# Batch 0's sine sums inside the thirds of x, step 1's P product ahead of step 0's Q product, joint E's last places two steps apart

## Chip, cores and metric

The kernel runs on one core of one Trainium2 chip. The metric is the device time of one execution in microseconds (us): the median over several runs. The core has five engines that work side by side, each through its own instructions in order: TensorE (PE in the profile; PEld are its weight loads), VectorE (DVE), ScalarE (ACT), GpSimd (POOL) and SyncE (SP), which here only issues DMAs. Matmul results land in PSUM, of which there are eight banks; all else is in SBUF.

## What is computed

```python
X = np.fft.fft(x, axis=1)            # x: (8, 3008, 256) float32
X = np.fft.fft(X, axis=2).real       # only the real part goes on
x = X.reshape(8 * 3008, 256)
gate = 1.0 / (1.0 + np.exp(-(x @ w_gate)))   # w_gate, w_val: (256, 1536)
val = x @ w_val
out = (gate * val) @ w_out                   # w_out: (1536, 256)
```

The three weights come in 64-bit floats and are turned into 32-bit ones on the chip. All matmuls are in 32-bit floats; each shows as two matmul pieces in the profile.

## The kernel before

**The algebra.** The transform over the 256 features is merged into the gate and value weights once: `merge` multiplies each chunk of 256 weight columns by the table `dt` and leaves the products in `G1` and `G2`. The transform over the 3008 rows is a cosine sum P (`pk`) and a sine sum Q (`qk`) over folded rows of x; a row k and its mirror row come out of the same two products, as G1·P plus and minus G2·Q. One feature (number 128) has its own cosine sums, called E (`er`, `ed`): they are added to the products through `ge`, in batch 0's first steps through a small matmul with `e0`.

**Batch 0's start** (lines 813 to 869). The rows of x come as a tile `X[0]` of 128 partitions with six slots q in each; the table `ST` holds, for each slot, the cosines and sines of 753 frequencies: first 377 even ones (NE), then 376 odd ones (NO). SP issues the loads in program order on one queue: two weight chunks, then three times two slots of x and the cosines of the same slots (lines 820 to 822), then the sines of slots 0 to 2 and of slots 3 to 5 (lines 823 and 824), then eight more weight chunks. A *third* is two slots. For each third `half_rows` (line 461) folds x on DVE (lines 405, 409, 418, 469, 471), and PE then runs the E sums (`pe`) and the cosine sums of both blocks: block 0 are the even, block 1 the odd frequencies, each in two PSUM tiles, `ev` and `od`, for even and odd slots. After the last third `then` (line 507) copies `ev` to SBUF on ACT (line 518), and `places` puts sum and difference of `ev` and `od` into `pk` with two DVE instructions (lines 524 and 528). The sine sums come after all thirds: slots 0 to 2 of block 0, then of block 1, then slots 3 to 5 of both (lines 857 to 860). Their results are placed into `qk` between the parts of weight chunks 2, 3 and 5.

**Weight chunks.** `weight_parts` is two ACT instructions (lines 296 and 297), `weight_join` three on DVE (306, 307, 309) and one on POOL (311), `weight_use` calls `merge`: four matmuls into a tile `ps` (eight pieces), two ACT copies (331, 332) and small DMAs. The order of chunks by `jobs` is such that step 0 uses chunk 2, step 1 chunks 3 and 5, step 2 chunk 6, step 3 chunk 8.

**Steps.** The main loop (line 942) has 576 steps; a step is one of 12 feature tiles f for one chunk of 252 rows k (six chunks in a batch). Step i has, in order of issue: `front_a` (PE: G1·P of gate and value into the bank `PF[i]`, and in steps 0 to 4 the E product with `e0` too), `gate_a(i-1)` (ACT 658, DVE 659), `part` (ACT 644: a copy of twice G1·P, into `ae`), `seed` (ACT 629: E for the next step), `gate_b(i-1)` (DVE 671, ACT 672, weight joins, DVE 675, POOL sums 681), `back` (PE: output products of step i−5), `front_b` (PE: G2·Q onto the same bank, which needs `part` to have read it), weight uses, then `n` entries from the list `later`, which `finish` fills every 12 steps with 24 entries (DVE sums, line 765, transposes, line 773, and stores), then whatever `at` put into `side` for this step.

**Joint E.** Steps 40 to 43 compute the E sums of the other seven batches: `e_joint` in step 40 (24 matmul pieces, two copies, two places), a copy in step 41, one place (line 524) in step 42, and the other place (line 528) and the store to `ed` in step 43.

Of the kernel before, what the change touches and what calls it, by code (L numbers as in the profile page):

```python
# [53 lines left out]
NQ = 6  # L54
NP = 128
# [26 lines left out]
def kernel(  # L82
# [10 lines left out]
    nc = tc.nc  # L93
    B, _, _, _, D = xf.shape
# [5 lines left out]
    NE = (M // 2) // 2 + 1  # L100
    NO = (M // 2) // 2
# [8 lines left out]
    N3 = NQ // 2  # L110
# [64 lines left out]
    ST = [const.tile([P, 2, NQ, NE + NO], F32, name="st", tag="st")]  # L175
# [11 lines left out]
    def load_rows(q, n):  # L187
        nc.sync.dma_start(out=X[0][0:NP, :, q : q + n], in_=xf[0, :, :, q : q + n])

    def load_table(t, q, n):  # L190
        nc.sync.dma_start(out=ST[0][0:NP, t, q : q + n], in_=stab[:, t, q : q + n])

    def table_again():

# [47 lines left out]
    def weight_load(j):  # L242


        w, c = jobs[j]
        src = (moe_w_gate, moe_w_val, moe_w_out)[w]
        src = src[2 * c * P : 2 * (c + 1) * P, :] if w == 2 else src[:, c * WC : (c + 1) * WC]
        src = src.rearrange("(c p) f -> p c f", p=P)

        def some(n, pool, tag):  # L250

            if tag not in shared:
                shared[tag] = pool.tile([P, n * WC], F32, name=f"w{tag}", tag=tag)
            return shared[tag]

        def home(j):

            if j in (0, 1, 2, 3, 5):
                if j > 2:
                    ws = some(5, pqp, "qk")[:, (j // 5) * 2 * WC : (j // 5 + 1) * 2 * WC]  # L260
                    return sp.tile([P, 4 * WC], F32, name="raw", tag="sf"), ws
                t = hp.tile([P, 6 * WC], F32, name="raw", tag="h")
                return t[:, 0 : 4 * WC], t[:, 4 * WC :]
            if j in (4, 6, 9):
                t = wf[:, {4: 1, 6: 2, 9: 3}[j]].rearrange("p m n -> p (m n)")
                return t[:, 0 : 4 * WC], t[:, 4 * WC : 6 * WC]
            t = some(10, cp, "c")
            if j == 7:
                raw = pqp.tile([P, 4 * WC], F32, name="raw", tag="pk")
                return raw, t[:, 6 * WC : 8 * WC]  # L270
            return t[:, 0 : 4 * WC], t[:, 4 * WC : 6 * WC]

        if j < KEEP:
            raw, ws = home(j)
        else:
            both = some(24, xp, "x4").rearrange("p (i n) -> p i n", n=2 * WC)
            r, i = (j - KEEP) % 3 * 2, 6 + (j - KEEP) % 6
            raw, ws = both[:, r : r + 2].rearrange("p a n -> p (a n)"), both[:, i]
            if w == 2:
                i = (0, 0, 8, 0, 2, 4)[c] * WC  # L280
                ws = some(10, cp, "c")[:, i : i + 2 * WC]
        raw = raw.bitcast(I32).rearrange("p (c f w) -> p c f w", c=2, w=2)
        ws = ws.rearrange("p (c f) -> p c f", c=2)
        WS[j] = ws
        if src.dtype == F32:
            nc.sync.dma_start(out=ws, in_=src)
        else:
            RAW[j] = raw
            nc.sync.dma_start(out=raw.rearrange("p c f w -> p c (f w)"), in_=src.bitcast(I32))

    def weight_parts(j):

        if j in RAW:
            raw, ws = RAW[j], WS[j]
            lo, hi = raw[:, :, :, 0], raw[:, :, :, 1]
            nc.scalar.activation(ws, hi.bitcast(F32), AF.Abs)
            nc.scalar.activation(lo, lo.bitcast(U32), AF.Copy, scale=2.0 ** -29)

    def weight_join(j):
        if j not in RAW:  # L300
            return
        raw, ws = RAW.pop(j), WS[j]
        lo, hi = raw[:, :, :, 0], raw[:, :, :, 1]
        wi = ws.bitcast(I32)
        ts = nc.vector.tensor_scalar
        ts(out=ws, in0=ws, scalar1=2.0 ** -15, scalar2=HUGE, op0=ALU.max, op1=ALU.min)
        ts(out=wi, in0=wi, scalar1=3, scalar2=0x3FFFFFF8, op0=ALU.logical_shift_left,
           op1=ALU.bitwise_and)
        nc.vector.scalar_tensor_tensor(out=wi, in0=hi, scalar=-(2 ** 30), in1=wi,
                                       op0=ALU.bitwise_and, op1=ALU.bitwise_or)  # L310
        nc.gpsimd.tensor_tensor(wi, wi, lo, op=ALU.add)
# [229 lines left out]
    def seq_group(b, blk, what, other=None):  # L541
        return half(b, lambda q: W[b, blk][what][:, q, :], PQE[b][what], blk, what == 1, other)
# [14 lines left out]
    def e_sums(m=B - 1):  # L557


        ps = bank("pe", NB - 1)  # L560
        at_ = lambda blk, par: slice((2 * blk + par) * TB, (2 * blk + par) * TB + m)

        def sums(*qs):
            for q in qs:
                for blk in range(2):
                    c0, n = ((0, NE), (NE, NO))[blk]
                    w = x8[:, :, 1 + 2 * blk, q] if m > 1 else W[0, blk][2][:, q]
                    mm(ps[at_(blk, q % 2), 0:n], w, ST[0][0:NP, 0, q, c0 : c0 + n], q < 2, q >= NQ - 2)

        def even():  # L570
            er = op.tile([P, NK + 1], F32, name="er", tag="os")[0:m]
            if m == 1:
                E0.append(er)
            nc.vector.memset(er[:, NK:], 0.0)
            a = evp.tile([P, 2 * NJ], F32, name="a", tag="a")[0:m, 0:NE]
            e1 = evp.tile([P, 2 * NJ], F32, name="a", tag="a")[0:m, 0:NE]
            nc.scalar.copy(a, ps[at_(0, 1), 0:NE])
            nc.scalar.copy(e1[:, 0:NO], ps[at_(1, 0), 0:NO])

            places(er, 0, True, a, ps[at_(0, 0), 0:NE])  # L580

            def rest():
                nc.scalar.copy(a[:, 0:NO], ps[at_(1, 1), 0:NO])

            def last():
                places(er, 1, False, e1[:, 0:NO], a[:, 0:NO], (0,))

            def end():
                places(er, 1, False, e1[:, 0:NO], a[:, 0:NO], (1,))
                nc.sync.dma_start(out=ed[1:] if m > 1 else ed[0:1], in_=er)  # L590
            return rest, last, end
        return sums, even
# [38 lines left out]
    def front_a(i):  # L631
        (pk, *_), ks, _, _, fs = cut(i)
        if i < N1:
            seed(i)
        for g in range(2):
            mm(PF[i][:, g], G1[:, g, fs], pk[:, ks], i < N1 and g == 0, True)
        for g in range(2 if i < N1 else 0):
            mm(PF[i][:, g], G2[:, g, fs], e0, False, True)

    def part(i):  # L640

        n = cut(i)[2]
        AP[i] = app.tile([P, 2, CH], F32, name="ae", tag="ae")[:, :, 0:n]
        nc.scalar.activation(AP[i], PF[i], AF.Copy, scale=2.0)  # L644
# [175 lines left out]
    for q in range(0, NQ, 2):  # L820
        load_rows(q, 2)
        load_table(0, q, 2)
    for q in range(0, NQ, N3):
        load_table(1, q, N3)
    for j in (2, 3, 5, 6, 8, 9, 4, 7):
        weight_load(j)

# [12 lines left out]

    cos = [seq_group(0, blk, 0, (2 * blk, 2 * blk + 1)) for blk in range(2)]
    e_, e_even = e_sums(1)
    for i, f in enumerate(fold_ops(0, 2)):
        q = 2 * i, 2 * i + 1
        f()
        e_(*q)
        cos[0][0](*q)
        cos[1][0](*q)
    cos[0][1]()()
    cos[1][1]()()  # L850
    rest, *ends = e_even()
# [2 lines left out]
    for f in ends:  # L854
        f()
    nc.scalar.copy(e0[0:1], E0[0][:, 0:CH])
    sin = [seq_group(0, blk, 1, (0, 1) if blk else None) for blk in range(2)]
    for q in range(0, NQ, N3):
        for sums, _, _ in sin:
            sums(*range(q, q + N3))  # L860
    for j in range(KEEP, KEEP + 3):
        weight_load(j)
    weight_join(2)
    weight_parts(3)
    sin[0][1]()()
    weight_parts(5)
    sin[1][1]()()
    weight_join(3)
    e_rows(0)
# [4 lines left out]
    def at(i, *fs):  # L874
        side.setdefault(i, []).extend(fs)
# [18 lines left out]
    i0 = NFT  # L894
    count = 3 * len(groups)
# [7 lines left out]
    later_e = []  # L903
# [1 line left out]
    at(3 * i0 + 5, lambda: later_e[0]())  # L905
    at(3 * i0 + 6, lambda: later_e[1]())
    at(3 * i0 + 6, table_again)
    at(3 * i0 + 7, lambda: later_e[2]())
    at(4 * i0 - 3, lambda: [at(i, f) for i, f in zip((50, 46, 48, 49, 51, 52), table_odd())])
    for i in range(i0, count, i0):  # L910
        at(i - (8 if i == i0 else 11), lambda i=i: e_rows(i))
# [28 lines left out]
    at((B - 2) * per + 4 * i0 + 8, lambda: [at((B - 2) * per + 4 * i0 + 9 + 2 * i, f) for i, f in enumerate(plain_ops())])  # L940

    for i in range(count):
        front_a(i)
        if i:
            gate_a(i - 1)
        part(i)
        if N1 <= i + 1 < count:
            seed(i + 1)
        if i:
            gate_b(i - 1, *join.pop(i, []))  # L950
        for f in pre.pop(i, []) + out_use.pop(i, []):
            f()
        if i >= 5:
            back((i - 5) // 3, (i - 5) % 3)
        merges = use.pop(i, [])
        for f in merges[0 : min(i, 1)]:
            f()
        front_b(i)
        for f in merges[min(i, 1) :]:
            f()  # L960
        n = 3 if i >= count - 8 else 2 + i % 2
        for f in later[0:n]:
            f()
        del later[0:n]
        for f in side.pop(i, []):
            f()
# [55 lines left out]
```

## Time and profile before

| what | value |
|---|---|
| runs, median (lowest to highest) | 1925.85 us (1925.78 to 1925.87) |
| profiled execution | 1925.74 us, of it the span on the core 1924.0 us |
| PE busy | 1910.2 us, 99% |
| DVE, ACT, POOL busy | 1430.1, 1343.0, 1522.6 us |
| 15 to 34 us (folding and sums of batch 0) | PE 17.66 of 19.0 us, DVE 14.91, DMA engines busy throughout, 399 GB/s |
| 34 to 48 us (steps 0 to 2) | PE 13.32 of 14.0 us, DVE 11.71, ACT 8.61, POOL 5.29 |
| 180 to 200 us (steps 40 to 45) | PE 18.81 of 20.0 us, DVE 16.17, POOL 17.58 |

How to read it: a busy share is the time in which the engine had an instruction at work, and says nothing of which engine the others wait for. That is told by the idle time of the engine that is on the path, with what ended each piece of it; the tables by stage show where engines are close to full. In the profile's lines a tile is named by its name in the program without its number, so `pf` is any `PF[i]`, and a matmul is written `out<-moving,stationary`. Line 134 is the helper that issues every matmul.

### The profile page before, as it was taken

What the parts mean: (1) busy time and instruction counts of PE and PEld (TensorE: products, weight loads), DVE (VectorE), ACT (ScalarE), POOL (GpSimd) and SP (SyncE); (2) the same over time, 40 slices, a digit from 0 to 9 for tenths busy, and PEclk for the clock granted to TensorE, in tenths of its full rate; (3) what the DMA queues carried; (4) which work ended last, traced back from release to release, by engine and by line L of the source; (5) the groups of instructions that cost most, each with busy time, mean ns of one, the idle gap of its engine ahead of it and who ended that gap; (6) DMA issues with size and microseconds to landing.
All of it is one profiled execution on the core that took longest, in us unless ns stands there. A gap on an engine that the chain in (4) does not pass through costs nothing.

```text
span 1924.0 us, 34205 instructions
## 1 busy us (share of the span) xinstructions
PE 1910.2 (99%) x11164; PEld 1776.2 (92%) x11164; DVE 1430.1 (74%) x3225; ACT 1343.0 (70%) x3148; POOL 1522.6 (79%) x2733
## 2 busy tenths in 40 slices
PE   8999999999999999999999999999999999999999
PEld 5789999999999999999999999999999999999998
DVE  7677877787777777777777777777777687777775
ACT  4877767767777677776777767777677767777775
POOL 2389969978898788986888878888788986877770
PEclk9999999999999999999999999999999999999999
DMA  8353222221131211202111121121200100011001
GB/s 312 106 99 74 72 80 57 51 66 29 20 77 26 80 18 35 70 14 80 26 47 50 20 82 21 47 51 24 80 15 15 26 16 15 14 21 21 15 17 31
DMA packets 172321, 97.02 MB, mean 50 GB/s; under 512 B 134397, under 2 KB 162792, under 8 KB 170096
## 3 DMA queue, kind: packets, MB, share of 16 engines
q1 hardware_dynamic: 171566, 94.32, 20.2%
q8 instruction: 90, 1.47, 0.3%
q14 instruction: 87, 0.71, 0.1%
q10 hardware_dynamic: 546, 0.51, 0.1%
q0 software_dynamic: 32, 0.00, 0.0%
HBM read 70.08 MB, written 46.71 MB: 61 GB/s over the span
## 4 chain that ended last, share of the span: by engine, by line
PE 97%; DVE 1%; ACT 0%; DMA 0%; issue 0%; SPq 0%
PE pf L134 51%; PE po L134 42%; PE ev L134 3%; PE ps L134 1%; PE od L134 1%; DMA raw<-in_moe_w_val_dram 0%; DVE c L765 0%; DVE x L418 0%; DVE x L469 0%; DVE z L659 0%; ACT ae L644 0%; PE pe L134 0%; ACT pf L672 0%; ACT wl L389 0%; DVE x L409 0%
## 5 line engine op out<-in xcount | busy, mean ns | idle before, releaser
L681 POOL TENSOR_TENSOR sf<-h 128x168 f32<-128x168 f32 (+1 forms) x920 | 510.2, 573 | 218.9 <-DVE h L675 218.6
L681 POOL TENSOR_TENSOR sf<-h,sf 128x168 f32<-128x168 f32 (+1 forms) x1104 | 614.8, 577 | 56.2 <-DVE h L675 55.7
L134 PE MATMUL pf<-qk,G 128*128 128x252 f32 (+1 forms) x2304 | 582.1, 375 | 1.9 <-ACT ae L644 1.9
L134 PE MATMUL pf<-pk,G 128*128 128x252 f32 (+1 forms) x2304 | 582.7, 376 | 0.0
L675 DVE TENSOR_TENSOR h<-pf,z 128x252 f32<-128x252 f32 (+1 forms) x576 | 241.6, 419 | 418.8 <-ACT pf L672 418.8
L629 ACT ACTIVATE pf<-ek,ge 128x252 f32<-128x252 f32 (+1 forms) x1142 | 538.0, 471 | 20.4 <-DMA ge<-G 1.1
L134 PE MATMUL po<-sf,wf 128*128 128x168 f32 (+1 forms) x2944 | 508.2, 305 | 0.0
L644 ACT ACTIVATE ae<-pf 128x504 f32<-128x504 f32 (+1 forms) x576 | 339.2, 589 | 237.7 <-PE pf L134 236.5
L134 PEld LDWEIGHTS pf<-pk,G 128*128 128x128 f32 x2304 | 436.8, 190 | 52.5 <-issue 2.3
L134 PEld LDWEIGHTS po<-sf,wf 128*128 128x128 f32 x2944 | 453.3, 190 | 8.0
L134 PE MATMUL po<-h,wf 128*128 128x168 f32 (+2 forms) x2584 | 459.7, 306 | 0.0
L134 PEld LDWEIGHTS pf<-qk,G 128*128 128x128 f32 x2304 | 411.0, 190 | 32.3 <-ACT ae L644 3.1
L765 DVE TENSOR_TENSOR c<-c 128x168 f32<-128x168 f32 (+1 forms) x920 | 431.0, 501 | 4.8
L134 PEld LDWEIGHTS po<-h,wf 128*128 128x128 f32 x2584 | 411.5, 190 | 17.0 <-issue 0.9
L659 DVE TENSOR_TENSOR z<-ae,pf 128x504 f32<-128x504 f32 (+1 forms) x576 | 383.7, 666 | 35.3 <-ACT h L658 33.7
L658 ACT ACTIVATE h<-pf 128x252 f32<-128x252 f32 (+1 forms) x576 | 217.8, 378 | 164.5 <-PE pf L134 158.7
L672 ACT ACTIVATE pf<-z 128x252 f32<-128x252 f32 (+1 forms) x576 | 214.0, 372 | 78.1 <-DVE h L671 75.0
L671 DVE TENSOR_TENSOR h<-h,pf 128x252 f32<-128x252 f32 (+1 forms) x576 | 232.9, 404 | 0.0
L681 POOL TENSOR_TENSOR sf<-sf 128x168 f32<-128x168 f32 (+1 forms) x184 | 105.5, 573 | 14.4
L681 POOL TENSOR_TENSOR sf<-sf,h 128x168 f32<-128x168 f32 (+1 forms) x184 | 100.3, 545 | 0.0
L748 ACT COPY c<-po 128x504 f32<-128x504 f32 (+1 forms) x138 | 78.4, 568 | 0.0
L773 DVE STREAM_TRANSPOSE os<-c 128x256 f32<-128x256 f32 x188 | 72.2, 422 | 0.4 <-issue 0.3
(139 smaller groups left out, 899.1 us busy)
## 6 DMA issues: line engine op xcount, KB each, us to landing
x<-xr SPq DMA_DIRECT2D x14, 1536.0 KB
out_dram<-os SPq DMA_DIRECT2D x368, 56.0 KB
xr<-in_xf_dram SPq DMA_DIRECT2D x14, 768.0 KB
xr<-in_xf_dram SPq DMA_DIRECT2D x35, 256.0 KB
ek<-ed SPq DMA_DIRECT2D x40, 126.0 KB
out_dram<-os SPq DMA_DIRECT2D x284, 7.0 KB
x<-in_xf_dram SPq DMA_DIRECT2D x3, 1024.0 KB
st<-in_stab_dram SPq DMA_DIRECT2D x3, 753.0 KB
```

Of the source, the lines that this page charges most:

```text
L134: nc.tensor.matmul(o, l, r, start=start, stop=stop, skip_group_check=True)
L629: nc.scalar.activation(PF[i][:, g], EK[i // NFT], AF.Copy, scale=ge[:, g, f : f + 1])
L644: nc.scalar.activation(AP[i], PF[i], AF.Copy, scale=2.0)
L658: nc.scalar.activation(H[p][:, fh, 0:n], PF[i][:, 0], AF.Sigmoid)
L659: nc.vector.tensor_tensor(z[:, :, ::-1], AP.pop(i), PF[i], op=ALU.subtract)
L671: nc.vector.tensor_tensor(h[:, fh, 0:n], h[:, fh, 0:n], pf[:, 1], op=ALU.mult)
L672: nc.scalar.activation(pf[:, 0], z[:, 0], AF.Sigmoid)
L675: nc.vector.tensor_tensor(h[:, fh, n:], pf[:, 0], z[:, 1], op=ALU.mult)
L681: nc.gpsimd.tensor_tensor(block(p, dst), block(p, a), block(p, b), op=(ALU.subtract, ALU.add)[op])
L748: (nc.vector.tensor_copy if t == 1 or t == 3 else nc.scalar.copy)(C[0][:, 3 * t * R : 3 * (t + 1) * R], PO[t][:, 0 : 3 * R])
L765: nc.vector.tensor_tensor(t[:, dst * R : (dst + 1) * R], *v, op=(ALU.subtract, ALU.add)[op])
L773: nc.vector.transpose(os_[0][:, s, 0:nb, h, :], t[:, c0 : c0 + nb * TB])
```

## The change

Three places of batch 0 are edited, and the table's loads with them.

The sines are loaded by blocks: behind the cosines of each two slots come the sines of the even block (377 columns) for the same slots, and the sines of the odd block (376 columns, all six slots) come in one load behind the last of these. Block 0's sine sums are run in each third, behind its cosine sums; block 1's sine sums follow after the thirds. The copy of block 0's sine sum on ACT is issued ahead of chunk 2's join, its two places on DVE behind it. Chunk 5's two ACT instructions move from ahead of block 1's places to behind `part(0)`.

In the loop `front_a(1)` is issued right behind `front_a(0)`, and step 1 has none.

Joint E's last place and its store go from step 43 to step 44, and steps 43 and 45 take two entries of `later` where odd steps take three.

```diff
-    def load_table(t, q, n):
-        nc.sync.dma_start(out=ST[0][0:NP, t, q : q + n], in_=stab[:, t, q : q + n])
+    def load_table(t, q, n, lo=0, hi=NE + NO):
+        nc.sync.dma_start(out=ST[0][0:NP, t, q : q + n, lo:hi], in_=stab[:, t, q : q + n, lo:hi])
...
     for q in range(0, NQ, 2):
         load_rows(q, 2)
         load_table(0, q, 2)
-    for q in range(0, NQ, N3):
-        load_table(1, q, N3)
+        load_table(1, q, 2, 0, NE)
+    load_table(1, 0, NQ, NE)
     for j in (2, 3, 5, 6, 8, 9, 4, 7):
         weight_load(j)
...
     cos = [seq_group(0, blk, 0, (2 * blk, 2 * blk + 1)) for blk in range(2)]
     e_, e_even = e_sums(1)
+    sin = [seq_group(0, 0, 1)]
     for i, f in enumerate(fold_ops(0, 2)):
         q = 2 * i, 2 * i + 1
         f()
         e_(*q)
         cos[0][0](*q)
         cos[1][0](*q)
+        sin[0][0](*q)
...
-    sin = [seq_group(0, blk, 1, (0, 1) if blk else None) for blk in range(2)]
-    for q in range(0, NQ, N3):
-        for sums, _, _ in sin:
-            sums(*range(q, q + N3))
+    sin.append(seq_group(0, 1, 1, (0, 1)))
+    sin[1][0](*range(NQ))
     for j in range(KEEP, KEEP + 3):
         weight_load(j)
+    places_0 = sin[0][1]()
     weight_join(2)
+    places_0()
     weight_parts(3)
-    sin[0][1]()()
-    weight_parts(5)
     sin[1][1]()()
     weight_join(3)
     e_rows(0)
...
-    at(3 * i0 + 7, lambda: later_e[2]())
+    at(3 * i0 + 8, lambda: later_e[2]())
...
     for i in range(count):
-        front_a(i)
+        if i != 1:
+            front_a(i)
+        if i == 0:
+            front_a(1)
         if i:
             gate_a(i - 1)
         part(i)
+        if i == 0:
+            weight_parts(5)
...
-        n = 3 if i >= count - 8 else 2 + i % 2
+        n = 3 if i >= count - 8 else 2 + (i % 2 and i not in (3 * i0 + 7, 3 * i0 + 9))
```

## What I predict, before the changed kernel ran

> **Where the time is.** I read the page first, then the list of waits by engine, then the timeline of each engine over the two places that the waits point to.
>
> ```profile
> span 1924.0 us, 34205 instructions
> ...
> PE 1910.2 (99%) x11164; PEld 1776.2 (92%) x11164; DVE 1430.1 (74%) x3225; ACT 1343.0 (70%) x3148; POOL 1522.6 (79%) x2733
> ...
> PE 97%; DVE 1%; ACT 0%; DMA 0%; issue 0%; SPq 0%
> ```
>
> TensorE bounds the kernel: 1910.2 of 1924.0 us busy, 97% of the chain that ended last, and the clock row of the page is 9 in every slice. The change takes no matmul out and puts none in, so all that it can win is idle time of PE. The waits of PE list that idle time whole:
>
> ```profile
> PE warm L134 <- DMA dt<-in_dtab_dram: 5.9, 1, 5.9
> PE pf L134 <- ACT ae L644: 1.9, 3, 1.1
> PE ev L134 <- DVE x L469: 1.3, 3, 0.6
> PE ps L134 <- POOL raw L311: 1.1, 1, 1.1
> ```
>
> The first and the last lie before any edited line (the first transform table, the second weight chunk). What is in reach is 1.9 + 1.3 us. PE's timeline places it (start, duration, then in brackets the idle time ahead of it and what ended it):
>
> ```profile
> 19.64 0.90 PE L134 MATMUL ev<-st,x 128*128 128x377 f32 x2 [0.58 <-DVE x L469]
> ...
> 23.75 0.90 PE L134 MATMUL ev<-st,x 128*128 128x377 f32 x2 [0.58 <-DVE x L469]
> ...
> 32.72 1.43 PE L134 MATMUL od<-st,x 128*128 128x376 f32 x4
> 33.98 1.01 PE L134 MATMUL pf<-pk,G 128*128 128x252 f32 x4
> ...
> 36.52 1.12 PE L134 MATMUL pf<-qk,G 128*128 128x252 f32 x4 [0.68 <-ACT ae L644]
> ...
> 199.04 1.12 PE L134 MATMUL pf<-qk,G 128*128 128x252 f32 x4 [1.06 <-ACT ae L644]
> ```
>
> So: 0.58 us before the second and before the third third of x, where PE is done with its cosines and VectorE (DVE) still folds; 0.68 us in step 0, where Q's product waits for ScalarE's copy; 1.06 us at 199.04, in step 45. A matmul that starts after idling takes 0.10 to 0.11 us more (0.90 against 0.80, 1.12 against 1.01). All of it together is 3.4 us of idle time and 0.4 us of such starts, some 3.8 us: a ceiling of 0.20%.
>
> **Part A, sines inside the thirds.** One row of a sum is two matmul pieces, 0.63 us (four rows from 23.75 to 26.39, with the late start). Each third now gets two rows more, 1.27 us, in place of 0.58 us of idle time, so by PE alone the third third would start with PE free at 24.72: 15.52, plus 2.73 for a late started third, 1.27 sines, 0.70 E rows, 2.53, 1.27, 0.70. But the order of the SP queue changes too. Half a sine third (377 of 753 columns, 0.386 MB) now goes ahead of the second part of x, and another ahead of the third. The semaphore events of the trace give when the loads of before landed: x 9.80, cosine 11.68, x 14.39, cosine 16.21, x 18.91, cosine 20.79, sine 23.50 and 26.25. A cosine third costs 1.82 to 1.88 us, half of one 0.93. So x lands at 15.32 and 20.77 instead of 14.39 and 18.91. DVE's timeline says when it wants them:
>
> ```profile
> 15.39 1.21 DVE L405 TENSOR_TENSOR x<-x 128x1020 f32<-128x1020 f32 x1
> ...
> 19.51 1.22 DVE L405 TENSOR_TENSOR x<-x 128x1020 f32<-128x1020 f32 x1
> ```
>
> The second part comes just in time (15.32 against 15.39), the third 1.26 us late. From DVE's start to PE's first cosine of that third were 23.75 − 19.51 = 4.24 us; 20.77 + 0.05 + 4.24 = 25.06, later than PE's 24.72, so DMA sets it. From there to the first pf were 33.98 − 23.75 = 10.23 us; four sine rows, 2.52 us, have gone ahead, leaving 7.71: pf at 32.77, a gain of 1.21. The halves are read in pieces of 1508 bytes, which the trace of before has nowhere. Its 2048-byte packets took 90 ns and the 6024-byte ones 237; scaled from the former, 16 pieces per queue engine take 1.05 us for each half, x lands at 21.0, and the gain is 0.97. I take 1.1, between the two. Bounds: x not late at all, 1.55 (pf at 24.72 + 7.71); a half as dear as a whole cosine third (1.85), x at 22.61, pf at 34.61, a loss of 0.63.
>
> The rule that speaks against these pieces is in the Trainium skill, "DMA: Bandwidth & Descriptors", section "How a descriptor splits into AXI transactions": a piece that doesn't start on a 256-byte boundary fetches bytes it doesn't use. By it I estimate four beats (32 bytes each) more on 47, 8% of each half, and a gain of about 1.05 instead of 1.21; that the trace's 1024-byte packets took 46 ns, 45 per KB against 40 for the 6024-byte ones, agrees in direction.
>
> **Part B, step 1's P ahead of step 0's Q.** Four P pieces and four of the E product, 1.70 us, stand between the P of step 0 and its Q, where ScalarE's copy (0.59 us, L644) needs 0.6: the wait of 0.68 and the late start of 0.11 go, 0.79 in all. This needs Q itself: its last DVE place (L528) ended at 35.35. With the third third 1.3 us later it, and the three DVE instructions of the weight join ahead of it, come to about 35.6; PE asks at 32.85 + 3.40 = 36.25. Bounds: 0.79 and, if Q is late, nothing.
>
> **Part C, joint E.** Step 43's DVE queue holds three later sums and E's last place:
>
> ```profile
> 193.93 2.15 DVE L765 TENSOR_TENSOR c<-c 128x168 f32<-128x168 f32 x3
> 196.00 0.88 DVE L528 TENSOR_TENSOR er<-a 7x376 f32<-7x376 f32 x1
> 196.81 0.66 DVE L659 TENSOR_TENSOR z<-ae,pf 128x504 f32<-128x504 f32 x1
> ```
>
> Behind them the z of L659, the gate L671, ScalarE's L672, L658 and L644 follow in turn, and PE's 199.04. One sum (0.72) and the place (0.81) leave step 43, so L659 comes 1.53 us earlier and L644 ends at about 197.5; PE asks at 197.98. The wait and its late start, 1.17, go. The place then sits in step 44 behind two sums (0.92 to 1.44), and L644 of step 46 ends at 200.8 to 201.6 against 201.13 for PE: up to 0.45 of it comes back. I take 1.05; bounds 1.17 and nothing. The two sums put off lengthen the list from step 49 to step 50, and the next finish is in step 52. E's store on SP goes a step later; the first row that is read from it is asked for in step 61.
>
> **Part D, what was covered.** PE reaches step 1 some 2 us earlier, the weights do not land earlier: the bytes ahead of them are the same.
>
> ```profile
> 37.09 1.36 POOL L311 TENSOR_TENSOR wqk<-wqk,raw 128x512 int32<-128x512 int32 x1 [3.30 <-DMA ge<-G]
> ...
> 49.04 1.29 POOL L311 TENSOR_TENSOR wc<-wc 128x512 int32<-128x512 int32 x1 [2.23 <-DVE wc L309]
> ```
>
> The first makes chunk 3, ready at 38.45, used by PE at 40.91; now PE asks at 38.83. Its DVE part starts after Q's last place, at 35.6, takes 1.6, and POOL 1.36: 38.6. The second makes chunk 8, ready at 50.33, used at 51.19; now asked for at 49.07 and, with DVE free of chunk 4's join at 45.1 (step 0's z at 39.83 plus the 5.27 us from there to L675's end as before), ready at 49.05. Both hold by 0.2 us or less, so I put in 0.15 lost; bounds 0 and 1.3 (chunk 8 no earlier than before). Moving chunk 5's two ScalarE passes (1.25 us) behind step 0's copy costs nothing: its chunk is ready at 41.1, PE asks at 41.4.
>
> A single-source DVE pass of the joins takes 0.43 us alone and 1.40 beside a POOL join (L307 at 37.33). The Trainium skill, "SBUF — State Buffer", section "Who interferes with whom", calls that an exclusive lock; by it one more such meeting would make the sum smaller by 0.97.
>
> **Sum**: 1.1 + 0.79 + 1.05 − 0.15 = 2.8 us. The profiled execution took 1925.74 us (span 1924.0, 1.7 around it), the median of the runs is 1925.85. 1925.85 − 2.8 = 1923.0 us, 0.15% less.
>
> **Rivals.** (1) *x isn't late* and all waits go: 1.55 + 0.79 + 1.17 = 3.5, 1922.3. For it: the pieces carry no more bytes; against it: x has only 0.6 us to spare in the third third and 0.93 goes ahead of it twice. (2) *The weight joins take the place of the idle time*: chunk 8 ready at 50.33 as before, so A and B together bring 51.19 − 50.33 = 0.86; with C 1.9, 1923.9. For it: two margins under 0.2 us; against it: DVE has gaps of 0.5 to 1.5 us from step 2 on. (3) *C only moves its wait* from step 45 to 46: 1.1 + 0.79 − 0.15 = 1.7, 1924.1. (4) *Slower: narrow sine rows at half rate.* The table's reload around 183 us has 3012-byte packets of 229 ns on average, though 118 at the least. If 1508-byte pieces cost double, the sines' 96 pieces per queue engine take 5.6 us more, and every weight behind them lands so much later: chunk 4 at 42.2 instead of 36.62. ScalarE stands in its queue before step 1's copy: 42.2 + 1.3 (its passes) + 1.5 (two copies, L658, L644) = 45.0, and PE's Q of step 1, at 42.63 before, comes 2.4 us later; with C, 1.3 slower: 1927.2. It decides from about 4.3 us of lateness; 8 us would make it 0.2%. Against it: the 229 ns were beside DRAM copies. For it: that part of the queue has no slack, and several joins hang on it.
>
> **Chances.** Forecast 0.55, (1) 0.10, (2) 0.12, (3) 0.08, (4) 0.15, two thirds of which with delays that cascade beyond 0.2%. The range is 1921.9 to 1925.4: it holds all but (4). Of the 0.2% (3.85 us) that a measurement of this kernel tells from no change, half of (1) at best comes near: faster 0.05, same 0.85, slower 0.10.
>
> **What would show it.** A: no idle before ev in the second third, 0.2 to 0.6 before the third's, pf near 32.9, L405's third start near 20.8 with a DMA as its releaser. B: no wait of qk behind L644 in step 0. C: none in step 45, under 0.5 in step 46. D: waits of ps on POOL L311 of at most 0.3. A first pf after 34, or a wait of ScalarE's L296 on a weight's DMA, would make me wrong.

## The result, and the profile after

The changed kernel takes 1923.06 us, the kernel before 1925.81 us (medians of 22 runs each, taken side by side; all runs of before lie between 1925.67 and 1925.94). The ratio is 0.9986, with a 95% interval of 0.998 to 0.9991: 2.75 us or 0.14% less, where 2.8 us less were forecast. One run of the changed kernel, 9513.87 us, is an outlier; the next highest is 1923.29. The profiled execution took 1923.16 us, so by the two profiled executions it is 2.58 us less.

The head of the page:

```profile
span 1921.4 us, 34211 instructions
...
PE 1910.5 (99%) x11164; PEld 1776.2 (92%) x11164; DVE 1429.4 (74%) x3225; ACT 1344.2 (70%) x3148; POOL 1524.8 (79%) x2733
```

PE's list of waits (who waited for whom: us in total, times, the longest):

```profile
PE warm L134 <- DMA dt<-in_dtab_dram: 5.8, 1, 5.8
PE ps L134 <- POOL raw L311: 1.0, 1, 1.0
PE ev L134 <- DVE x L471: 0.4, 2, 0.2
PE ps L134 <- POOL wc L311: 0.2, 1, 0.2
PE pf L134 <- ACT ae L644: 0.2, 1, 0.2
```

PE does the same work in the same time, 1910 us; its waits on ScalarE's copy are down from 1.9 to 0.2, those on the fold from 1.3 to 0.4, and one wait is new, 0.2 for a weight join (`wc`). The 0.2 left on ScalarE's copy lies past 1000 us and was there before. PE's timeline shows where they stand:

```profile
20.25 0.90 PE L134 MATMUL ev<-st,x 128*128 128x377 f32 x2
...
25.25 0.90 PE L134 MATMUL ev<-st,x 128*128 128x377 f32 x2 [0.19 <-DVE x L471]
...
32.94 1.01 PE L134 MATMUL pf<-pk,G 128*128 128x252 f32 x4
...
36.34 1.01 PE L134 MATMUL pf<-qk,G 128*128 128x252 f32 x4
...
49.57 0.70 PE L134 MATMUL ps<-wc,dt 128*128 128x256 f32 x2 [0.16 <-POOL wc L311]
```

The second third starts without a wait, the third with 0.19 left; the first pf is at 32.94 instead of 33.98; Q's product of step 0 follows step 1's P with no wait; in step 3 PE waits for chunk 8. DVE's timeline gives the reason for the third third, the late rows of x, which before had no wait there at all:

```profile
21.00 1.22 DVE L405 TENSOR_TENSOR x<-x 128x1020 f32<-128x1020 f32 x1 [1.38 <-DMA x<-in_xf_dram]
```

The gain can be followed along the kernel by setting the starts of Q's products of each step, before minus after: 1.96 us in step 1, 1.51 from step 3 on, 2.74 in step 45, 2.64 and 2.51 in steps 46 and 47, 2.41 at the end of PE's work, 2.58 at the end of the span. Between steps 3 and 45 and from step 47 to step 112 nothing moves; in step 112 a tenth goes, and no experiment ties it to one edit.

### The profile page after: what moved, and what is told of

The parts are those of the page before. It is cut to its first block, busy times and chain, and to the rows that moved or that the text cites. A ratio compares the mean times of both kernels' runs of the same rounds, so it can differ in the third digit from the quotient of the medians.

```text
span 1921.4 us, 34211 instructions
## 1 busy us (share of the span) xinstructions
PE 1910.5 (99%) x11164; PEld 1776.2 (92%) x11164; DVE 1429.4 (74%) x3225; ACT 1344.2 (70%) x3148; POOL 1524.8 (79%) x2733
## 4 chain that ended last, share of the span: by engine, by line
PE 98%; DMA 1%; DVE 1%; ACT 0%; issue 0%; SPq 0%; ACTq 0%
PE pf L134 51%; PE po L134 43%; PE ev L134 3%; DMA x<-in_xf_dram 1%; PE od L134 1%; PE ps L134 1%; DMA raw<-in_moe_w_val_dram 0%; PE pe L134 0%; DVE z L659 0%; DVE wf L307 0%; ACT wl L389 0%; DVE x L418 0%; DVE x L469 0%; DVE x L405 0%; ACT ae L644 0%
```

## Experiments

All kernels were run in turn with the kernel before on one chip for each group; differences are of medians to the kernel before in the same group, whose median was between 1925.63 and 1925.91. The intervals of the ratios are about 0.09% wide to each side, so the sign of the smaller differences isn't settled by them alone; each of the medians below is of 11 runs (8 for one), the runs of a kernel and of the one before do not overlap in any group, and the traces place the differences.

| kernel | median, us | minus before | ratio and interval |
|---|---|---|---|
| only A | 1924.45 | −1.25 | 0.9994 (0.9985 to 1.0003) |
| only B | 1925.16 | −0.54 | 0.9997 (0.9988 to 1.0006) |
| only C | 1924.63 | −1.07 | 0.9994 (0.9986 to 1.0003) |
| only the loads of A | 1927.06 | +1.36 | 1.0007 (0.9998 to 1.0016) |
| after, loads of before | 1930.55 | +4.68 | 1.0025 (1.0015 to 1.0035) |
| after, half sines behind x | 1922.81 | −3.06 | 0.9984 (0.9975 to 0.9993) |
| after, chunk 4 in steps 3 and 4 | 1924.18 | −1.69 | 0.9991 (0.9982 to 1.0) |
| the last two together | 1923.91 | −1.96 | 0.999 (0.9981 to 0.9999) |
| after, E's place back in step 43 | 1923.61 | −2.30 | 0.9988 (0.9979 to 0.9998) |
| after, three entries again | 1923.68 | −2.23 | 0.9989 (0.998 to 0.9998) |
| after, chunk 5's passes back | 1924.20 | −1.71 | 0.9991 (0.9983 to 1.0) |
| half sines behind x, chunk 4's join in step 3 | 1922.26 | −3.37 | 0.9983 (0.9974 to 0.9992) |

**Each part alone.** The theory is that the three parts remove three separate waits of PE and add up. Only A is the changed kernel without these:

```diff
-        if i != 1:
-            front_a(i)
-        if i == 0:
-            front_a(1)
+        front_a(i)
...
-    at(3 * i0 + 8, lambda: later_e[2]())
+    at(3 * i0 + 7, lambda: later_e[2]())
...
-        n = 3 if i >= count - 8 else 2 + (i % 2 and i not in (3 * i0 + 7, 3 * i0 + 9))
+        n = 3 if i >= count - 8 else 2 + i % 2
```

> The sines inside the thirds, the loads by blocks and the moved weight passes, without B (step 1's P stays in step 1) and without C. My theory, that the parts add up: the first pf at about 32.9 us as in the changed kernel, the waits of qk in step 0 (0.7) and step 45 (1.1) still there, no wait of ps on POOL in step 3, and 1.0 us less than before: 1924.8. The rival, that A lives only together with B because PE would just wait for Q instead: 1925.5 or more.

Only B is the kernel before with the first of these edits, only C the kernel before with the other two.

> Only step 1's P product ahead of step 0's Q product. My theory: the idle 0.68 us before qk in step 0 goes with its late start, about 0.9 us by PE's starts, and some 0.1 to 0.2 of it comes back as a wait of ps on POOL in step 3, where 0.86 us of margin are asked for 0.92: 1925.0. The rival, that Q is ready in time only because A has put its sums earlier: a wait of qk on DVE in step 0 and 1925.6 to 1925.9.

> Only joint E's last place in step 44 and two entries of the list in steps 43 and 45. My theory: the wait of step 45 goes, 0.1 to 0.2 comes back in steps 46 and 47, 1.0 us less: 1924.8. The rival, that the wait moves to step 46: 1925.8.

Alone they bring 1.25, 0.54 and 1.07 us, 2.86 in sum, against 2.75 together: they add up within what the medians can tell. In the trace of only A the two waits behind ScalarE's copy are still there (0.68 and 1.08 us), and none on POOL in step 3. (A brings 0.25 more than the 1.0 expected; 0.17 of it lies behind PE's last matmul, see the account of the terms below.) Only B has no wait in step 0, a gain of 0.92 by Q's start in step 1 and 0.53 from step 3 on: chunk 8 is late there too, by more than I expected (0.35 of starts for 0.08 us of listed idle time). So Q is ready without A, and the loss in step 3 belongs to B rather than to A and B together. Only C leaves no wait in step 45.

**What the cut of the loads costs by itself.** The kernel before with the new loads alone:

```diff
-    for q in range(0, NQ, N3):
-        load_table(1, q, N3)
+        load_table(1, q, 2, 0, NE)
+    load_table(1, 0, NQ, NE)
```

> Only the order and cut of the table's loads of the changed kernel; all sums where they were before. My theory: x of the third third lands 2.0 us later (20.9 us), DVE folds it 1.4 us later and PE's cosines and all behind them come 1.4 to 1.5 us later: 1927.3. The rival, that pieces of 1508 bytes run at half rate: x lands at 23 us or later, 1929 or more. A second rival, that the fold is not held by this load: 1925.8.

1.36 us more than before. The third part of x lands at 21.04 us by the semaphore events, DVE waits 1.42 for it, and PE's third third starts at 25.31 instead of 23.75:

```profile
21.06 1.22 DVE L405 TENSOR_TENSOR x<-x 128x1020 f32<-128x1020 f32 x1 [1.42 <-DMA x<-in_xf_dram]
```

A half third of the sines takes 1.00 to 1.06 us from the landing ahead of it to its own. So half rate is out, and the price of the queue's new order is 1.4 us by the medians and 1.55 by PE's starts, paid inside part A out of the 2.5 us of sines that no longer stand behind the thirds.

**The new order of the sums without the new loads.** The changed kernel with the two loads of before:

> The changed kernel with the loads of before: sines of slots 0 to 2, then of slots 3 to 5, behind all of x and the cosines. My theory: PE stands in the first third until the first sines land at 23.5 us, everything behind it in its queue with it, the first pf comes near 37.7 us instead of 32.9, the wait of ps on POOL in step 3 goes, and the time is 4.2 to 4.8 us above the changed kernel: 1927.5. The rival, that the cut of the loads is worth nothing: 1923.1.

1930.55, or 7.4 us above the changed kernel, 2.6 more than my upper figure. The wait is where I had it, once, 5.37 us for the first sines. But afterwards PE itself is slow. Three stretches of this kernel (busy time and count of PE, PEld, DVE, ACT and POOL, then the granted clock, DMA share and GB/s):

```profile
14.00:24.00 10.00, 4.44 (x20) 2.07 (x19) 9.35 (x18) 0.65 (x2) 0.00 (x0) 0.86 1.02 412
24.00:34.00 10.00, 10.00 (x36) 4.19 (x36) 0.00 (x0) 0.40 (x1) 0.00 (x0) 0.80 1.04 389
34.00:44.00 10.00, 10.00 (x39) 7.04 (x38) 8.14 (x18) 7.11 (x16) 1.30 (x1) 1.00 0.46 150
```

and two rows of its PE timeline:

```profile
23.68 1.60 PE L134 MATMUL ev<-st,x 128*128 128x377 f32 x2 [5.37 <-DVE x L471]
25.07 1.46 PE L134 MATMUL od<-st,x 128*128 128x377 f32 x2
```

Two pieces take 1.46 us where they take 0.80 elsewhere, and the clock of the stretch is 0.80; the trace's clock events have it at one half from 21.2 to 28.1 us. All eight runs of this kernel have a mean clock of 0.998 or 0.999, where every run of the others has 1.0. My sum had counted the wait and not what it does to the clock. (The wait is listed under DVE L471, which was long done at 23.68; it was the sines' DMA, which landed at 23.54.) One part of the theory failed: the wait of `ps` on POOL in step 3 did not go. It costs 0.43 us of starts here too, though PE gets there 7.4 us later than in the changed kernel and the load of chunk 8 (`wc`) is issued earlier, at 18.96 us instead of 22.44. So the load isn't what makes chunk 8 late.

**Is the third third held by the load of x?** The changed kernel with each half of the sines behind the x rows of the next third:

```diff
-    for q in range(0, NQ, 2):
-        load_rows(q, 2)
-        load_table(0, q, 2)
-        load_table(1, q, 2, 0, NE)
+    load_rows(0, 2)
+    load_table(0, 0, 2)
+    for q in range(2, NQ, 2):
+        load_rows(q, 2)
+        load_table(1, q - 2, 2, 0, NE)
+        load_table(0, q, 2)
+    load_table(1, NQ - 2, 2, 0, NE)
```

> The changed kernel with each half of the sines issued behind the x rows of the next third instead of ahead of them (x, cosines, x, sines of the third before, cosines, and so on). My theory, that DMA sets the third third in the changed kernel: x of that third lands near 20.0 us instead of 20.97, DVE waits 0.4 instead of 1.38, PE goes from the E sums of that third straight into its cosines near 24.9 instead of 25.25 with a late start, first pf near 32.5, 0.3 to 0.45 less: 1922.7. The rival, that DVE's fold is just as long as PE's work and the load doesn't matter: 1923.1.

The third fold in its DVE timeline:

```profile
19.94 1.22 DVE L405 TENSOR_TENSOR x<-x 128x1020 f32<-128x1020 f32 x1 [0.39 <-DMA x<-in_xf_dram]
```

DVE waits 0.39 instead of 1.38, PE starts the third at 24.95 with no listed wait, 0.74 behind the start of the E rows as in the second third, the first pf is at 32.65; the difference to before is 3.06 instead of 2.75. The load was what held it.

**What makes chunk 8 late.** My theory was chunk 4's join on DVE ahead of step 1's z. First try, its ScalarE passes in step 3 and its join in step 4:

```diff
-    for j, i in ((5, 0), (6, 1), (4, 1), (8, 2), (9, 3), (10, 4), (11, 5), (7, 5), (12, 6), (13, 7), (14, 8),
+    for j, i in ((5, 0), (6, 1), (8, 2), (9, 3), (4, 4), (10, 4), (11, 5), (7, 5), (12, 6), (13, 7), (14, 8),
```

> The changed kernel with weight chunk 4's parts and join moved from steps 0 and 1 to steps 3 and 4 (it is used in step 5). My theory, that chunk 4's join on DVE ahead of step 1's z makes chunk 8 late in step 3: the wait of ps on POOL at 49.6 goes with its late start, 0.45 less: 1922.6. The rival, that chunk 8 is late by its own ScalarE passes or its load: 1923.1 and the wait still there.

> The changed kernel with both: the sines behind the x rows of the next third, and chunk 4's join in step 4. My theory, that the two are independent: 0.75 to 0.9 less than the changed kernel, 1922.25. The rival, that an earlier start in step 0 only makes another weight chunk late: 1922.6 to 1922.7.

Neither helped: 1924.18 and 1923.91, 1.06 and 1.10 us above the kernels that they were made from, each as its difference to before. The wait in step 3 did go, and from step 2 to step 3 Q's product gains 0.43 us; but step 5 loses 1.5, as the PE timeline of the first of them shows:

```profile
57.41 1.96 PE L134 MATMUL po<-h,wf 128*128 128x504 f32 x4 [0.41 <-POOL wf L311]
59.94 1.99 PE L134 MATMUL ps<-wx,dt 128*128 128x256 f32 x8 [0.57 <-POOL wx L311]
```

The join of chunk 4 was now the late one (`wf`, an output weight, used in step 5), and chunk 10's join behind it too (`wx`): on DVE the two joins of step 4 ran from 54.26 to 58.37. So the cause in step 3 was right and the new place wrong. The last kernel moves only the join, to step 3 behind chunk 9's, on top of the reordered loads:

```diff
-    for j, i in ((5, 0), (6, 1), (4, 1), (8, 2), (9, 3), (10, 4), (11, 5), (7, 5), (12, 6), (13, 7), (14, 8),
+    for j, i in ((5, 0), (6, 1), (8, 2), (9, 3), (4, 3), (10, 4), (11, 5), (7, 5), (12, 6), (13, 7), (14, 8),
...
-            pre.setdefault(i - 1, []).append(lambda j=j: weight_parts(j))
+            pre.setdefault(0 if j == 4 else i - 1, []).append(lambda j=j: weight_parts(j))
```

> The kernel with the sines behind the x rows of the next third, and of chunk 4 only the join moved, to step 3 behind chunk 9's join; its ScalarE passes stay in step 0, and step 4 keeps chunk 10's join alone. My theory, that moving chunk 4's join out of step 1 frees DVE for chunk 8 and that what was lost in step 5 came from its stay beside chunk 10's join in step 4: no wait of ps or po on POOL in steps 3 and 5, and 0.3 to 0.4 below the kernel with only the loads reordered (1922.81): 1922.45. The rival, that any later place of chunk 4's join makes chunk 10 or the output weights late: 1922.9 or more, with a wait of ps or po on POOL in step 5.

PE's list of waits in this kernel:

```profile
PE warm L134 <- DMA dt<-in_dtab_dram: 5.9, 1, 5.9
PE ps L134 <- POOL raw L311: 0.9, 1, 0.9
PE ev L134 <- DVE x L471: 0.2, 1, 0.2
PE pf L134 <- ACT ae L644: 0.2, 1, 0.2
```

No wait on POOL is left but the one at 12.7 us, and from step 2 to step 3 Q's product loses nothing, where the kernel with only the loads reordered loses 0.36. The difference to before is 3.37 us: the fastest of all, 0.6 us better than the changed kernel, and 0.31 better than with only the loads reordered, where 0.3 to 0.4 were expected.

**Which edit of C does it.** The changed kernel with `later_e[2]` back in step 43, and the changed kernel with `2 + i % 2` entries again:

> The changed kernel with joint E's last place and its store back in step 43; the list still gives two entries in steps 43 and 45. My theory, that the wait of step 45 is the sum of what stands on DVE in step 43 (one list entry 0.72, the place 0.81): z comes 0.8 us later, a wait of 0.5 to 0.7 of qk in step 45 with its late start, less what steps 46 and 47 no longer lose: 0.5 to 0.8 above the changed kernel, 1923.7. The rival, that the shorter list alone removes the wait: 1923.1.

> The changed kernel with three list entries in steps 43 and 45 again; the place stays in step 44. My theory: z of step 43 comes 0.7 us later, a wait of 0.4 to 0.6 in step 45, and the place then delays step 46 as well: 0.7 to 1.2 above the changed kernel, 1924.0. The rival, that moving the place alone removes the wait: 1923.1.

Each brings the wait of step 45 back in part. The line of it in PE's list of waits, with E's place back in step 43:

```profile
PE pf L134 <- ACT ae L644: 0.7, 2, 0.6
```

and with three entries again:

```profile
PE pf L134 <- ACT ae L644: 0.5, 2, 0.4
```

Set against the steps ahead, Q's product of step 45 starts 0.73 and 0.52 us later than in the changed kernel. By the medians they lose 0.45 and 0.52 of the 1.07 of part C, less than the 0.5 and 0.7 that I had as the least: neither edit alone is enough, and the two losses together are about the whole.

**Chunk 5's passes.** The changed kernel with `weight_parts(5)` back ahead of block 1's places:

> The changed kernel with chunk 5's two ScalarE passes back ahead of block 1's sine copy. My theory: they hold that copy and the copy of step 0 (L644) 1.1 us, Q is placed near 36.9 instead of 35.8 and PE, which asks at 36.3, waits 0.5 to 0.7 with a late start: 0.6 to 0.9 above the changed kernel, 1923.8. The rival, that there is slack there (in the prediction I put the move at nothing): 1923.1.

1.04 us above the changed kernel. The cause I gave is the smaller part: counted from the first pf, Q's product of step 0 starts 0.27 us later than in the changed kernel (0.10 of it listed as idle time). Q's places on DVE are late, chunk 3's join behind them too, and PE stands in step 1, which by the starts of Q's products loses another 0.87:

```profile
39.86 1.35 PE L134 MATMUL ps<-wqk,dt 128*128 128x256 f32 x5 [0.56 <-POOL wqk L311]
```

## Why the prediction was right

**What bounds the kernel** held: PE is as busy as before (1910.5 us against 1910.2), and what was won is idle time, 2.75 us. The ceiling of 3.8 us was added up wrongly: the waits listed are 1.9 and 1.3, so 3.2 us and not 3.4, and 0.35 of them (the first third's and the one past 1000 us) stand where nothing was edited. Part B shows what speaks the other way, that a gap is longer than listed.

**Part A**: forecast 1.1, measured 1.04 (first pf from 33.98 to 32.94). The steps were right one by one: x of the third third forecast between 20.77 and 21.0, landed at 20.97; DVE's fold started at 21.00 with that DMA as its releaser; PE's cosines forecast at 25.06, measured 25.25; the reordered loads show that it was the load. What was off is the time at which PE alone would be ready: 24.72 in the sum, 24.95 in the kernel with the reordered loads, where DVE no longer holds it. The price of a 1508-byte half, put between 0.93 and 1.05, was 0.99 to 1.05 from the landing ahead of it: the 8% that the Trainium skill's section on descriptors and AXI transactions ("DMA: Bandwidth & Descriptors") gave as my estimate lies within these 6 to 13%.

**Part B**: forecast 0.79, measured 0.92 by the start of Q's product in step 1. The mechanism held (Q was ready: its last place ended at 35.79, and the next DVE instruction began at 35.70; the 35.35 of before from which the forecast of 35.6 was made is such a begin, the place itself ended at 35.44); the term was too small because I took the listed 0.68 us for the whole wait. The step before ended its issue at 35.68: eight pieces from 33.98 on, 0.85 for each four. PE stood 0.84 us, of which the listing shows 0.68, since the end of the last piece is drawn some 0.16 later than the next one could start. With the late start of 0.11 that is 0.95; 0.03 of it went on step 1's weight product, 1.92 us instead of 1.89.

**Part C**: forecast 1.05, measured 1.23 in step 45, of which 0.10 and 0.13 came back in steps 46 and 47, 1.0 in all. E's place in step 44 did make step 46 late, as the term "up to 0.45" had it. DVE's timeline of the changed kernel has the new order:

```profile
192.51 1.56 DVE L765 TENSOR_TENSOR c<-c 128x168 f32<-128x168 f32 x2
...
196.61 0.88 DVE L528 TENSOR_TENSOR er<-a 7x376 f32<-7x376 f32 x1
```

**Part D**: forecast a loss of 0.15, measured 0.45. This is the term that was mis-sized most. Chunk 3 was as worked out, ready at 38.79 (forecast 38.6) for a use at 38.92. Chunk 8 was ready at 49.52 where I had 49.05: step 0's z began at 40.08 instead of 39.83. Of these 0.25, 0.09 are Q's product, which began at 36.34 instead of 36.25, and 0.16 the copies of `ps` on ScalarE: the first began at 39.12, behind the drawn end of `ps` at 39.08, and not at 38.92, when PE went on to its next product. Then two of the first passes of joins took 0.51 and 0.55 us instead of 0.42, both started beside a POOL join. PE asked at 49.24, and here too the listed 0.16 stand for 0.33 us and a late start. "Both hold by 0.2 us or less" was the place to put more than 0.15. That the move of chunk 5's passes "costs nothing" is not wrong but too little: it is worth 1.0 us, as passes in their old place would have made chunk 3 late in the new order.

The errors of the terms, −0.06, +0.13, −0.05 and −0.30, leave 2.5 us by PE's starts instead of 2.8. That the medians show 2.75 is due to what lies outside them: 0.1 lost in step 112, 0.17 won between the last matmul and the end of the span, and 0.17 that the medians differ more than the two profiled executions. The second goes with the loads: 0.16 or 0.17 are won there in the trace of every kernel with the new loads, also of the one that has nothing but the loads, and at most 0.01 in the three with the loads of before (only B, only C, the new sums with the old loads). How the loads do it isn't shown, and no run explains the other two. So that the total came out closer than its terms is luck.

**The rivals.** (1) x not late: refuted by DVE's wait of 1.38. What it would have brought is seen with the reordered loads: the first pf came 1.33 earlier than before, not 1.55, since PE itself is ready only at 24.95. (2) The joins take the place of the idle time: it happened at the spot named, chunk 8 in step 3, at 0.45 us where the rival had 1.0 (0.86 instead of 1.89 for A and B). (3) C only moves its wait: refuted, 0.23 of 1.23 moved. (4) Narrow rows at half rate: refuted by the landings, 0.99 to 1.06 us where half rate asked for some 1.9.

## What to carry to other kernels

When an engine is busy 99% of the time, list its idle gaps with what ended each; their sum, with what the listing leaves out, is the ceiling, and here each gap could be worked on alone. A gap of the matmul engine costs more than the listing shows (here 0.68 stood for 0.95 and 0.16 for 0.45), so small new waits count for a multiple of what is listed. Work that is moved earlier moves its loads earlier too: issue them behind the loads that another engine waits for first; and a join that is moved out of the way has to stay early enough for its own use and for the join behind it: chunk 4's cost 1.5 us in step 4, ahead of chunk 10's, and nothing in step 3, behind chunk 9's.

## What the runs showed of the hardware

A wait of 5.4 us in PE's queue halved the granted clock: 0.5 from 21.2 to 28.1 us, 6.8 us of it, though PE had work again from 23.68 on. Of the 7.4 us that the kernel with the old loads lost to the changed one, 5.5 are the wait for the sines (from 18.15 to 23.68), and 2.1 the slow clock: from there to the first pf it took 16.67 us (23.68 to 40.35), the changed kernel 14.79 (18.15 to 32.94), of which 0.26 were the wait of its third third, that the other has not. Once the clock was at 1.0 (from 9.3 to 11.0 us on in the traces), the waits of all other runs, 1.4 us at the longest, left it there to the end of the work. The Trainium skill, "TensorE: Matmul & The Clock Gate", section "Part 1: The HAM clock gate (the "warmup" mystery)", has the half rate after an idle window of about 3.4 us. The trace agrees in size, but the window was not idle throughout: the clock fell 2.9 us after the drawn end of PE's last piece (18.30). The time at half rate is two such windows, 6.83 us, and the time at 1.0 ahead of it three, 10.24 us. Counted so, the window before the fall began at 17.82, when PE still had up to half a microsecond of work, and about one microsecond of work (23.68 to 24.64) in the first slow window did not end the half rate; it ended with the next window, in which PE was at work throughout. This is one trace; the mean clock of one of the eight runs, 0.999, would fit a single slow window.
